# Batch 0 turned to kappa rows by DMA transposes in place of identity products, in a Fourier mixing layer followed by an expert layer on one core

## The chip, the cores and the metric

The kernel runs on 1 core of one Trainium2 chip. The metric is the device time of one execution in microseconds, as the median of several runs. Before the change it is 860.0 us.

## The reference

Input `x` has 8 batches of 3008 positions with 256 channels. Each batch goes through a Fourier transform along the positions, a complex product with two 256x256 matrices, a soft threshold and the inverse transform. The 24064 rows that come out go through a dense layer of 2048 hidden units with a squared ReLU. Cut to what matters:

```python
X = np.fft.rfft(x, axis=1)                 # x: 8 x 3008 x 256
Yr = Xr @ w_r - Xi @ w_i + b_r
Yi = Xr @ w_i + Xi @ w_r + b_i
Yr = np.sign(Yr) * np.maximum(np.abs(Yr) - 0.01, 0.0)   # Yi likewise
y = np.fft.irfft(Yr + 1j * Yi, n=3008, axis=1)
h = y.reshape(24064, 256) @ w_in           # 256 x 2048
g = s * np.maximum(h, 0.0) ** 2 + b
out = g @ w_out                            # 2048 x 256
```

## The kernel before

**The transform as products.** 3008 is split as 94 x 32 (`N1`, `N2`). A first small product over the 94 (matrix `A_t`) gives 96 "kappa" rows for each of the 32 positions n2. Then comes a product over the 32 n2 for each of 24 pairs of frequencies (`F_t`), the mixing with the weights (`W_t`, `W_g`), the threshold, the product back (`T_t`), and a last product over the 96 kappa rows (`C_t`), which gives the 94 again. Between these products the data must be turned, so that the index to be summed lies on the partitions. TensorE (PE) does the products into PSUM, ScalarE (ACT) and VectorE (DVE) copy them out ("evictions"), GpSimd (POOL) issues the loads of `x` and of the expert weights, and SyncE (SP) issues all other transfers.

**Batch 0, the prologue** (`first_batch`, line 351). Nothing else can fill the engines yet, so batch 0 has a path of its own. Its first step (line 362) leaves `ut` in SBUF, with channels on the partitions. Then it goes in 12 steps (ec, u): two halves of the channels (ec, 128 each) by `U` = 6 groups of four pairs. Step i emits, in this order: `mix` of step i (line 411, eviction to g at 418 or 421), `fwd_dft` of step i-1 (line 442, threshold at 447 on ACT and 449 on DVE, giving z), `inv_dft` of step i-2 (line 460, eviction into `vt`). `vt` holds, for a half, channels on the partitions and 96 kappa values for each of 32 n2. When the six steps of a half are through, `turn(ec, k)` turns eight n2 at a time to kappa rows: eight products of a 128x96 block of `vt` with an identity (line 474), and one eviction of 96x1024 elements into `vs[0]`. `last_dft(ec, n2)` (line 489) then does the last product for eight n2 and evicts it to `yt`, which the expert layer reads. The four turns of the first half lie among the steps of the second; the four of the second half stand behind them:

```python
            k = i - U - 2
            if 0 <= k < 4:
                turn(0, k)
            if 0 <= k - 1 < 4:
                last_dft(0, 8 * (k - 1))
            if i >= 2 * U:
                some(3)
...
        for k in range(4):
            turn(1, k)
            some(1)
            if k:
                last_dft(1, 8 * (k - 1))
        last_dft(1, 24)
        return more
```

`some(n)` emits n of the 16 units of batch 1's first step (`s1_units`, line 550; products at 564), each four products and one eviction of 128x384 elements into `u`. Ten of the 16 are emitted here, and the other six among tile 0 of the expert layer (`schedule(0, 10, more)`, line 865).

**Batches 1 to 7.** Here the result `u` of the first step is turned by DMA transposes, one for each half of the channels, as soon as eight units are through (line 574, issued by SP): `us` <- `u`, 24 blocks of 128x128. `s23_units` (line 582) goes on from there with `fwd_unit` (products at 597), mixing (612, 626), threshold (631 to 638), small copies through `ring`, `inv_unit` (656), and a way through memory (`vd`, line 665, read back as `vs`, line 672). `s4_units` (line 693) is the last product.

**The expert layer.** 48 tiles of at most 512 rows are worked through in order. Each has 16 slots; a slot emits `first_mm` (line 758, ReLU on ACT at 765 and the square on DVE at 772 or ACT at 769) and its share of `second_mms` of the tile before (line 829, scaled and stored at 839 and 784). The work of the later batches is laid into these slots by hand in `plan`: `s23_units(1)` starts at slot 24, that is in the middle of tile 1; slot 17 loads `x` of batch 2, gated by a one-element copy that waits for the first transposed half of batch 1 (line 185).

**What sets the order.** Each engine works through its own instructions in the order of the program, and waits for semaphores. PSUM has three pools of two buffers: `psh` (two banks each, `two_banks`), `psf` (`one_bank`) and `psa` (`other_bank`). `evac` (line 155) gives each eviction to ACT or DVE, whichever has the smaller sum of estimated work so far; the sums are set to zero after `first_batch`. The loads of the prologue run in this order on POOL: `x` of batch 0; then, gated by the arrival of the table `T_c`, `x` of batch 1, `w_in` (line 266) and `w_out` (line 267).

Of the kernel before, what the change touches and what calls it, by code (L numbers as in the profile page):

```python
# [9 lines left out]
F16 = mybir.dt.float16  # L10
F32 = mybir.dt.float32
# [3 lines left out]
P = 128  # L15
N1 = 94
N2 = 32
# [79 lines left out]
def kernel(  # L97
# [13 lines left out]
    nc = tc.nc  # L111
    B, S, D = x.shape
    N = S
    assert N == N1 * N2 and D == 2 * P and B % 2 == 0
    DC = D // P
# [3 lines left out]
    HW = N2 // 2  # L119
# [7 lines left out]
    sel = np.zeros((P, P))  # L127
    sel[0, :64] = 1.0
    sel[64, 64:] = 1.0
    E_d = nc.inline_tensor(np.eye(P).astype(np.float16), name="identity").ap()  # L130
    S_d = nc.inline_tensor(sel.astype(np.float16), name="bias_sel").ap()

    cpool = ctx.enter_context(tc.tile_pool(name="consts", bufs=1))
    bigpool = ctx.enter_context(tc.tile_pool(name="big", bufs=1))
# [12 lines left out]
    tpool = ctx.enter_context(tc.tile_pool(name="tp", bufs=2))  # L147
# [7 lines left out]
    def evac(dst, src, cols, scale=None):  # L155
        ta, td = 0.17 + cols / 1200.0, 0.15 + cols / 960.0
        if load["act"] + ta <= load["dve"] + td:
            load["act"] += ta
            if scale is None:
                return None, nc.scalar.copy(out=dst, in_=src)  # L160
            return None, nc.scalar.mul(out=dst, in_=src, mul=scale)
        load["dve"] += td
        if scale is None:
            return nc.vector.tensor_copy(out=dst, in_=src), None
        return nc.vector.tensor_scalar_mul(out=dst, in0=src, scalar1=scale), None

    def two_banks():
        return hpool.tile([P, 2, 512], F32, name="psh", tag="psh")

    def one_bank():  # L170
        return fpool.tile([P, 512], F32, name="psf", tag="psf")

    def other_bank():
        return apool.tile([P, 512], F32, name="psa", tag="psa")
# [38 lines left out]
        nc.sync.dma_start(out=st, in_=w.rearrange("(c p) e -> p c e", p=P))  # L213
        w_st.append(st)

    b_g = cpool.tile([P, 2, D], F32, name="b_g")
    nc.vector.memset(b_g, 0.0)
    for r in (0, 64):
        for i, bv in enumerate((b_r, b_i)):
# [2 lines left out]
    F_c = first_c[:, 0].rearrange("p (q r k) -> p q r k", q=NPAIR, r=2)  # L222
    T_c = first_c[:, 1].rearrange("p (q k) -> p q k", q=NPAIR)
    F_2 = [first_c[:, 2 + i].rearrange("p (q k) -> p q k", q=H) for i in range(2)]
    b_h = cpool.tile([P, D], F16, name="b_h")
    nc.vector.memset(b_h, 0.0)

    for i, bv in enumerate((b_r, b_i)):
        nc.gpsimd.dma_start(out=b_h[64 * i : 64 * i + 1], in_=bv.unsqueeze(0))
    sel_t = cpool.tile([P, P], F16, name="sel_t")  # L230
    eye_t = cpool.tile([P, P], F16, name="eye_t")
    C_t = cpool.tile([96, 96], F16, name="C_t")

    b_st = rpool.tile([P, 2, D], F32, name="b_st", tag="rt")
# [12 lines left out]
    def emit_load_inverse():  # L247
        nc.sync.dma_start(
            out=F_c[:, H:].rearrange("p q r k -> p q (r k)"), in_=F_d[:, H:]
        )  # L250
        t_load = nc.sync.dma_start(out=T_c, in_=T_d)
        with tc.issue_after(t_load.ins):
            nc.sync.dma_start(out=eye_t, in_=E_d)
            nc.sync.dma_start(out=C_t, in_=C_d)
            for i, bv in enumerate((b_r, b_i)):
                nc.sync.dma_start(out=b_st[:, i], in_=bv.unsqueeze(0).to_broadcast([P, D]))
            nc.sync.dma_start(out=s_bc, in_=moe_s.unsqueeze(0).to_broadcast([P, 1]))
            nc.sync.dma_start(out=bb_bc, in_=moe_b.unsqueeze(0).to_broadcast([P, 1]))
# [67 lines left out]
    def sum_w_out():  # L326
        acc = opool.tile([P, 2, D], F32, name="acc", tag="ost")
        nc.gpsimd.tensor_tensor(
            out=acc, in0=w_out_t[:, 0:2], in1=w_out_t[:, 2:4], op=ALU.add
        )  # L330
        for q in range(4, MC, 2):
            nc.gpsimd.tensor_tensor(out=acc, in0=acc, in1=w_out_t[:, q : q + 2], op=ALU.add)
        nc.gpsimd.tensor_tensor(out=w_sum, in0=acc[:, 0], in1=acc[:, 1], op=ALU.add)

    def make_bias():
        ps = other_bank()
        nc.tensor.matmul(ps[:, 0:D], ones, w_sum, start=True, stop=True)
        for j in range(2):
            nc.scalar.activation(
                out=bias_bc[:, j], in_=ps[:, 0:D], func=AF.Copy, scale=bb_bc  # L340
            )

    us = {}
    vs = {}
    ring = []
# [5 lines left out]
    def first_batch():  # L351
# [3 lines left out]
        for g in range(N2 // 4):  # L355
            c, h = divmod(g, 2)
            for dc in range(DC):
                ps = one_bank() if dc else two_banks()[:, 0]
                with tc.issue_after(last_pe.ins):
                    for j in range(4):  # L360
# [4 lines left out]
                            start=True, stop=True,  # L365
# [32 lines left out]


        U = NPAIR // 4  # L400
        vt = bigpool.tile([P, DC, N2, 96], F16, name="vt", tag="corr")
        gs = {}
        zt = {}
        g_last = [None]
# [1 line left out]
        def mix(ec, u):  # L406
            ps = two_banks().rearrange("p h (j r e) -> p (h j) r e", j=2, r=2)
            for j in range(4):
                q = 4 * u + j
                for dc in range(DC):  # L410
                    nc.tensor.matmul(  # L411
                        ps[:, j], ut[:, dc, 4 * q : 4 * q + 4, :],
                        W_t[:, dc, :, ec * P : (ec + 1) * P],
                        start=(dc == 0), stop=(dc == DC - 1),
                    )
            g = vpool.tile([P, 4, 2, P], F16, name="g0", tag="v")
            if u % 3 == 1:
                g_last[0] = nc.scalar.copy(out=g, in_=ps)
                load["act"] += 1.02
            else:  # L420
                g_last[0] = nc.vector.tensor_tensor(
                    out=g, in0=ps,
                    in1=b_g[:, :, ec * P : (ec + 1) * P].unsqueeze(1).to_broadcast([P, 4, 2, P]),
                    op=ALU.add,
                )
                load["dve"] += 1.2
            gs[(ec, u)] = g
# [40 lines left out]

        vs[0] = vspool.tile([P, N2, D], F16, name="vs", tag="vs")

        def turn(ec, k):
            ps = two_banks()
            for j in range(8):
                nc.tensor.matmul(
                    ps[0:96, j // 4, (j % 4) * P : (j % 4) * P + P],
                    vt[:, ec, 8 * k + j, :], eye_t, start=True, stop=True,
                )
            evac(
                vs[0][0:96, 8 * k : 8 * k + 8, ec * P : (ec + 1) * P],
                ps[0:96].rearrange("p h (j e) -> p (h j) e", e=P), 1024,  # L480
            )

        yt = yts[0] = ypool.tile([P, DC, N2, 96], F16, name="yt", tag="yt")

        def last_dft(ec, n2):

            ps = [one_bank(), other_bank()]
            for j in range(8):
                nc.tensor.matmul(
                    ps[j // 4][:, (j % 4) * 96 : (j % 4) * 96 + 96],  # L490
                    vs[0][0:96, n2 + j, ec * P : (ec + 1) * P], C_t,
                    start=True, stop=True,
                )
            for i in range(2):
                evac(
                    yt[:, ec, n2 + 4 * i : n2 + 4 * i + 4, :],
                    ps[i][:, 0:384].rearrange("p (j n) -> p j n", n=96), 384,
                )

        more = s1_units(1, True)  # L500

        def some(n):
            for _ in range(n):
                if more:
                    more.pop(0)()

        steps = [(ec, u) for ec in range(DC) for u in range(U)]
        for i in range(2 * U + 2):
            if i < 2 * U:
                mix(*steps[i])  # L510
            if 0 <= i - 1 < 2 * U:
                fwd_dft(*steps[i - 1])
            if 0 <= i - 2 < 2 * U:
                inv_dft(*steps[i - 2])
            k = i - U - 2
            if 0 <= k < 4:
                turn(0, k)
            if 0 <= k - 1 < 4:
                last_dft(0, 8 * (k - 1))
            if i >= 2 * U:  # L520
                some(3)
            if i == 0:
                with tc.issue_after(g_last[0].ins):
                    place_t(0)
            if i == 1:
                with tc.issue_after(g_last[0].ins):
                    place_f(1)
            if i == 2:
                with tc.issue_after(g_last[0].ins):
                    place_f_2(1)  # L530
            if i == 3:
                with tc.issue_after(g_last[0].ins):
                    place_t(1)
            if i == 9:

                gate = nc.gpsimd.tensor_copy(out=low[0:1, 0, 0:1], in_=vt[0:1, 1, 0, 0:1])
                with tc.issue_after(gate.ins):
                    make_w_g()
                    make_bounds()
                    sum_w_out()  # L540
        for k in range(4):
            turn(1, k)
            some(1)
            if k:
                last_dft(1, 8 * (k - 1))
        last_dft(1, 24)
        return more


# [302 lines left out]
    def schedule(start, span, units):  # L852
        for i, u in enumerate(units):
            plan.setdefault(start + (i * span) // len(units), []).append(u)

    more = first_batch()
    load.update(act=0.0, dve=0.0)
    def load_x_2():
# [3 lines left out]
    for i, tl in enumerate(tiles):  # L862
        if tl[0] == "main" and tl[2] == 0 or tl[0] == "wide" and tl[2] == (0, 0):
            mark[tl[1]] = i * MC
    schedule(0, 10, more)
    plan.setdefault(15, []).append(make_bias)
    plan.setdefault(17, []).append(load_x_2)
    schedule(24, 42, s23_units(1))
# [1 line left out]
    for b in range(2, B):  # L870
        s0, s1, s2 = mark[b - 2], mark[b - 1], mark[b]
        p = s1 - s0
        schedule(s0 + 40, p - 48, s1_units(b))
        p = s2 - s1
# [47 lines left out]
```

## Time and profile before

| what | value |
|---|---|
| runs | 859.21, 860.0, 860.82 us; median 860.0 |
| the profiled execution | 860.82 us, of which its span is 859.0 us |
| granted TensorE clock | 0.994 of full speed on average |
| busy share of the span | PE 97%, PE weight loads 71%, DVE 81%, ACT 74%, POOL 5% |
| chain that ended last | PE 86%, DMA 7%, ACT 3%, DVE 2% |
| identity products (line 474) | 64, of 219 ns each, overlapping; 8 in 0.61 us |
| evictions of the turns | 6 on ACT of 1013 ns, 2 on DVE of 1214 ns |
| transposes of line 574 | 14; SP held for 3.6 to 15.8 us each, median 4.8 |
| first expert product | at 49.1 us |

"Span" is the time from the first to the last instruction of the core; the profiled execution takes 1.8 us beyond it. A busy PE is not a PE at its peak, since products are pipelined and their ends modelled. The shares are means over stages with different limits. "Wait" is idle time of an engine with what released it. SP's own time is not in the busy table; how long one instruction holds SP's queue is read in the timeline.

### The profile page before, as it was taken

How to read it: one execution, taken by the hardware profiler on the slowest of the kernel's cores; microseconds unless marked ns; L12 is line 12 of the kernel's file. 1: busy time of each engine (PE TensorE's matmuls, PEld its weight loads, DVE VectorE, ACT ScalarE, POOL GpSimd, SP SyncE). 2: the span in 40 equal slices, each digit the busy share in tenths (PEclk: the TensorE clock that was granted, in tenths of full speed). 3: DMA queues.
4: the chain of work that ended last, by engine and by line, in shares of the span. 5: the costliest groups of instructions: out<-in, count | busy, mean ns of one | idle time of the engine just before them, and what ended most of it. 6: DMA issues, size and time to landing. Idle time of an engine off the chain costs nothing.

```text
span 859.0 us, 17659 instructions
## 1 busy us (share of the span) xinstructions
PE 833.9 (97%) x6981; PEld 608.6 (71%) x6981; DVE 694.0 (81%) x1025; ACT 638.9 (74%) x858; POOL 46.5 (5%) x72
## 2 busy tenths in 40 slices
PE   8899999999999999799989999999999999999997
PEld 6766777777777766477767777777767777766765
DVE  6888987888878987588968888788887888776674
ACT  5887877788778877478767777687877878766673
POOL 5440000000000001000000000000000000000000
PEclk9999999999999999899999999999999999999999
DMA  7862368122851359422682226813262132411111
GB/s 171 151 117 73 86 157 179 41 77 72 198 128 46 101 148 121 78 73 81 120 168 69 71 82 140 181 38 89 79 171 63 50 87 81 128 33 38 38 44 50
DMA packets 123829, 84.11 MB, mean 98 GB/s; under 512 B 52070, under 2 KB 118634, under 8 KB 122402
## 3 DMA queue, kind: packets, MB, share of 16 engines
q1 hardware_dynamic: 117298, 68.56, 32.4%
q0 software_dynamic: 6448, 14.42, 10.4%
q8 instruction: 55, 0.90, 0.4%
q14 instruction: 28, 0.23, 0.1%
HBM read 41.53 MB, written 35.65 MB: 90 GB/s over the span
## 4 chain that ended last, share of the span: by engine, by line
PE 86%; DMA 7%; ACT 3%; DVE 2%; issue 1%; POOL 0%; SPq 0%; DVEq 0%; ACTq 0%; POOLq 0%
PE psa L829 36%; PE psh L758 35%; PE psf L626 4%; DMA us<-u 3%; PE psf L597 2%; PE psf L612 2%; PE psf L656 2%; PE psf L564 2%; PE psf L707 2%; DMA vs<-vd 1%; DMA x<-in_x_dram 1%; ACT rt L765 1%; DMA ring<-ring 1%; DMA vd<-v 1%; PE psh L411 1%
## 5 line engine op out<-in xcount | busy, mean ns | idle before, releaser
L765 ACT ACTIVATE rt<-psh 128x1024 f32<-128x1024 f32 (+2 forms) x384 | 387.3, 1010 | 117.9 <-PE psh L758 115.6
L772 DVE TENSOR_TENSOR gt<-rt 128x1024 f16<-128x1024 f32 (+2 forms) x320 | 383.8, 1204 | 98.0 <-ACT rt L765 97.0
L829 PE MATMUL psa<-w_out_t,gt 128*128 128x256 f16 (+1 forms) x3024 | 455.8, 273 | 0.0
L829 PEld LDWEIGHTS <-gt 128*128 128x128 f16 (+1 forms) x3024 | 301.3, 101 | 185.3 <-issue 1.4
L758 PE MATMUL psh<-yt,w_in 128*128 128x512 f16 (+1 forms) x1344 | 398.2, 378 | 0.2 <-ACT rt L765 0.2
L758 PEld LDWEIGHTS <-w_in 128*128 128x128 f16 x1536 | 138.0, 98 | 14.3 <-issue 0.5
L839 DVE SCALAR_TENSOR_TENSOR ost<-psa,s_bc,bias_bc 128x512 f32<-128x512 f32 (+2 forms) x97 | 71.1, 733 | 14.3 <-PE psa L829 10.5
L769 ACT ACTIVATE gt<-rt 128x1024 f16<-128x1024 f32 (+2 forms) x64 | 67.4, 1054 | 1.0
L160 ACT CAST v<-psf 128x512 f16<-128x512 f32 x80 | 46.6, 583 | 22.5 <-PE psf L656 22.4
L160 ACT CAST xf<-psf 128x512 f16<-128x512 f32 x77 | 45.0, 586 | 19.7 <-PE psf L597 19.7
L631 DVE TENSOR_TENSOR ring<-psf,s 128x512 f16<-128x512 f32 x84 | 57.5, 685 | 2.6 <-PE psf L626 2.4
L758 PE MATMUL psh<-tail,w_in 128*128 128x512 f16 (+1 forms) x192 | 52.6, 355 | 0.0
L160 ACT CAST u<-psf 128x384 f16<-128x384 f32 x85 | 40.8, 481 | 13.6 <-PE psf L564 12.8
L626 PE MATMUL psf<-W_g,xf 128*128 128x256 f16 x336 | 50.4, 272 | 0.1
L160 ACT CAST yt<-psf 128x480 f16<-128x480 f32 (+2 forms) x68 | 34.9, 532 | 13.7 <-PE psf L707 13.5
L189 POOL DMA_DIRECT2D x<-in_x_dram x36 | 18.8, 527 | 454.2 <-PE psf L564 452.7
L597 PE MATMUL psf<-F_t,us 128*128 128x128 f16 x336 | 33.3, 221 | 8.4 <-DMA us<-u 8.4
L637 DVE TENSOR_TENSOR ring<-ring,high 128x512 f16<-128x512 f16 x84 | 35.5, 423 | 2.3
L638 DVE TENSOR_TENSOR ring<-ring 128x512 f16<-128x512 f16 x84 | 35.6, 423 | 2.2
L636 DVE TENSOR_TENSOR ring<-ring,low 128x512 f16<-128x512 f16 x84 | 35.4, 422 | 1.7
L707 PE MATMUL psf<-C_t,vs 96*128 96x96 f16 x448 | 33.9, 208 | 2.5 <-DMA vs<-vd 2.4
L564 PEld LDWEIGHTS <-x 94*128 94x128 f16 x448 | 30.8, 98 | 7.2 <-issue 3.4
(89 smaller groups left out, 518.2 us busy)
## 6 DMA issues: line engine op xcount, KB each, us to landing
out_dram<-ost SPq DMA_DIRECT2D x152, 128.0 KB
vd<-v SPq DMA_DIRECT2D x42, 256.0 KB
vs<-vd SPq DMA_DIRECT2D x14, 768.0 KB
x<-in_x_dram POOLq DMA_DIRECT2D x28, 376.0 KB, 6.8
ring<-ring SPq DMA_DIRECT2D x280, 32.0 KB
out_dram<-ost SPq DMA_DIRECT2D x16, 120.0 KB
x<-in_x_dram POOLq DMA_DIRECT2D x8, 188.0 KB, 6.4
out_dram<-ost SPq DMA_DIRECT2D x12, 112.0 KB
```

Source lines behind the costliest of these rows:

```text
L160: return None, nc.scalar.copy(out=dst, in_=src)
L564: nc.tensor.matmul(ps[:, j * 96 : j * 96 + 96], x16[(b, c)][0:N1, lo : lo + P], A_t[0:N1, :], start=True, stop=True,)
L597: nc.tensor.matmul(ps[:, :, dc, j, :], us[b][:, 2 * i + j, dc * P : (dc + 1) * P], F_t[:, 2 * i + j, :], start=True, stop=True,)
L626: nc.tensor.matmul(ps[:, r, :], xt[:, 2 - r, dc], W_g[:, dc, r], start=(dc == 0), stop=(dc == DC - 1),)
L631: nc.vector.tensor_tensor(out=t, in0=ps, in1=hold[i // 2][:, i % 2].unsqueeze(1).to_broadcast([P, 2, D]), op=ALU.add,)
L707: nc.tensor.matmul(ps[:, j * 96 : (j + 1) * 96], vs[b][0:96, n2 + j, ec * P : (ec + 1) * P], C_t, start=True, stop=True,)
L758: nc.tensor.matmul(o, w_in_t[dc][:, mc * P : (mc + 1) * P], r, start=(dc == 0), stop=(dc == DC - 1),)
L765: nc.scalar.activation(out=rt[:, :, 0:w], in_=ps[:, :, 0:w], func=AF.Relu)
L769: nc.scalar.activation(out=gt[:, :, 0:w], in_=rt[:, :, 0:w], func=AF.Square)
L772: nc.vector.tensor_tensor(out=gt[:, :, 0:w], in0=rt[:, :, 0:w], in1=rt[:, :, 0:w], op=ALU.mult)
L829: nc.tensor.matmul(ps[0:size, h, :], gts[(ti, mc // 2)][:, mc % 2, sub * size : (sub + 1) * size], w_out_t[:, mc, :], start=(mc == 0), sto ...
L839: nc.vector.scalar_tensor_tensor(out=ost[0:size, 0:k], in0=ps[0:size, 0:k], scalar=s_bc[0:size], in1=bias_bc[0:size, 0:k], op0=ALU.mult, o ...
```

## The change

`turn` no longer uses TensorE. It issues two DMA transposes on SP for each half of the channels, 16 n2 each, from `vt` straight into `vs[0]`. The source block must be 128 wide for this, so `vt` gets 128 instead of 96 columns for each n2, and the padding is set to zero by a memset on POOL at the start. To make room, the identity is no longer loaded, and three small constants (`b_g`, `b_h`, `sel_t`) move to a pool that is used only later. The transposes of the first half are emitted once its six steps are through, and those of the second likewise. The calls of `last_dft(0, ...)` stand one step later than before, at i = 10 to 13. All 16 units of batch 1's first step are now emitted in the prologue: twelve behind the last step, and four among the calls of `last_dft(1, ...)`. The diff, without the lines that only move constants:

```diff
+    vt = bigpool.tile([P, DC, N2, P], F16, name="vt", tag="corr")
+    nc.gpsimd.memset(vt[:, :, :, 96:P], 0.0)
...
-        vt = bigpool.tile([P, DC, N2, 96], F16, name="vt", tag="corr")
...
-        def turn(ec, k):
-            ps = two_banks()
-            for j in range(8):
-                nc.tensor.matmul(
-                    ps[0:96, j // 4, (j % 4) * P : (j % 4) * P + P],
-                    vt[:, ec, 8 * k + j, :], eye_t, start=True, stop=True,
-                )
-            evac(
-                vs[0][0:96, 8 * k : 8 * k + 8, ec * P : (ec + 1) * P],
-                ps[0:96].rearrange("p h (j e) -> p (h j) e", e=P), 1024,
-            )
+        def turn(ec):
+
+            for k in range(2):
+                nc.sync.dma_start(
+                    out=vs[0][:, HW * k : HW * k + HW, ec * P : (ec + 1) * P],
+                    in_=vt[:, ec, HW * k : HW * k + HW].rearrange("p n k -> p (n k)"),
+                    transpose=True,
+                )
...
-            k = i - U - 2
-            if 0 <= k < 4:
-                turn(0, k)
-            if 0 <= k - 1 < 4:
-                last_dft(0, 8 * (k - 1))
-            if i >= 2 * U:
-                some(3)
+            if i - 1 in (U, 2 * U):
+                turn((i - 1) // U - 1)
+            if 0 <= i - U - 4 < 4:
+                last_dft(0, 8 * (i - U - 4))
...
+        some(12)
         for k in range(4):
-            turn(1, k)
+            last_dft(1, 8 * k)
             some(1)
-            if k:
-                last_dft(1, 8 * (k - 1))
-        last_dft(1, 24)
         return more
...
-    schedule(0, 10, more)
+    assert not more
```

More of the change, by code (lines that the diff above doesn't have):

```diff
@@ L129 @@
     sel[64, 64:] = 1.0
-    E_d = nc.inline_tensor(np.eye(P).astype(np.float16), name="identity").ap()
     S_d = nc.inline_tensor(sel.astype(np.float16), name="bias_sel").ap()
@@ L214 @@
         w_st.append(st)
-    b_g = cpool.tile([P, 2, D], F32, name="b_g")
+    b_g = tpool.tile([P, 2, D], F32, name="b_g", tag="tail")
     nc.vector.memset(b_g, 0.0)
@@ L224 @@
     F_2 = [first_c[:, 2 + i].rearrange("p (q k) -> p q k", q=H) for i in range(2)]
-    b_h = cpool.tile([P, D], F16, name="b_h")
+    sb_t = tpool.tile([P, P + D], F16, name="sb_t", tag="tail")
+    sel_t, b_h = sb_t[:, 0:P], sb_t[:, P:]
     nc.vector.memset(b_h, 0.0)
@@ L229 @@
         nc.gpsimd.dma_start(out=b_h[64 * i : 64 * i + 1], in_=bv.unsqueeze(0))
-    sel_t = cpool.tile([P, P], F16, name="sel_t")
-    eye_t = cpool.tile([P, P], F16, name="eye_t")
     C_t = cpool.tile([96, 96], F16, name="C_t")
@@ L252, in emit_load_inverse @@
         with tc.issue_after(t_load.ins):
-            nc.sync.dma_start(out=eye_t, in_=E_d)
             nc.sync.dma_start(out=C_t, in_=C_d)
```

## The prediction

> **What bounds the kernel now.** I read the page first: span, busy shares, chain of waits.
>
> ```profile
> span 859.0 us, 17659 instructions
> PE 833.9 (97%) x6981; PEld 608.6 (71%) x6981; DVE 694.0 (81%) x1025; ACT 638.9 (74%) x858; POOL 46.5 (5%) x72
> ...
> PE 86%; DMA 7%; ACT 3%; DVE 2%; issue 1%; POOL 0%; SPq 0%; DVEq 0%; ACTq 0%; POOLq 0%
> ```
>
> TensorE sets the time over the whole span. But the change touches only batch 0's prologue, so I read that stretch by itself (columns: stretch, length, busy PE, PEld, DVE, ACT, POOL, clock, DMA share, GB/s).
>
> ```profile
> 30.00:35.00 5.00, 4.58 (x64) 4.01 (x63) 3.90 (x5) 4.12 (x7) 2.49 (x3) 1.00 1.28 197
> 35.00:40.00 5.00, 4.93 (x73) 4.47 (x72) 4.77 (x7) 4.41 (x9) 3.63 (x5) 1.00 0.65 90
> 40.00:45.00 5.00, 3.54 (x59) 2.94 (x56) 4.47 (x10) 3.92 (x9) 4.69 (x5) 1.00 0.02 5
> 45.00:50.00 5.00, 4.49 (x75) 3.58 (x73) 4.12 (x7) 4.80 (x8) 3.33 (x4) 1.00 0.40 76
> ```
>
> From 30 to 50 us no engine is the bound alone: PE, DVE and ACT each work 70 to 99% and pass PSUM banks round. The DMA queues are full until 37 us and empty from 38 to 48. After 70 us PE is busy without a gap, so what counts is how much later or earlier PE enters that state. Next I read the transposes that the kernel already has (line 574, 24 blocks of 128x128 each), in the timeline:
>
> ```profile
> 46.88 3.78 SPq L574 DMA_TRANSPOSE us<-u  x1
> ...
> 52.60 1.00 POOL L185 COPY x<-us 1x1 f16<-1x1 f16 x2 [4.04 <-DMA us<-u]
> ...
> 56.10 9.38 SPq L574 DMA_TRANSPOSE us<-u  x1
> ...
> 67.55 0.51 PE L597 MATMUL psf<-F_t,us 128*128 128x128 f16 x6 [1.77 <-DMA us<-u]
> ```
>
> With empty queues one transpose holds SP 3.8 us and lands 5.7 us after its issue; beside the load of x it lands after 11.4 us, and PE idles 1.8 us for it.
>
> **What is removed.** The identity products and their evictions:
>
> ```profile
> L474 PE MATMUL psh<-eye_t,vt 128*96 128x128 f16 x64 | 4.9, 219 | 0.0
> ...
> L160 ACT CAST vs<-psh 96x1024 f16<-96x1024 f32 x6 | 6.1, 1013 | 0.1
> ...
> L164 DVE CAST vs<-psh 96x1024 f16<-96x1024 f32 x2 | 2.4, 1214 | 0.5 <-PE psh L474 0.5
> ```
>
> That is 4.9 us of PE and 8.5 us of ACT and DVE together, 4.3 us if it splits evenly. None of it comes out as such: what stands in its place are waits for transfers.
>
> **What is added.** Four transposes of 16 blocks on SP, two for each channel half (ec), with nothing but loads ahead of them there. By the free row the data starts 1.2 us after issue, 24 blocks take 3.7 us and the release 0.7 us. So 16 blocks take 2.4 us: one lands 4.4 us after issue (1.2+2.5+0.7), a second behind it 2.4 us later.
>
> *First pair.* Its input, `vt` of ec 0, is complete at 31.0 us (ACT's eviction of 30.43, which the change does not move), so it is issued at 31.1. The queues are then full with the load of w_out:
>
> ```profile
> q0 software_dynamic: 2069, 1.19, 131.2%
> ...
> q0 software_dynamic: 365, 1.21, 86.2%
> q1 hardware_dynamic: 721, 0.18, 19.3%
> ```
>
> The first line is 31 to 37.4 us, the others 57.3 to 64.7 us, where a transpose (q1) ran beside the load of x (q0): two transpose packets passed for each packet of the load. w_out's packets are small, 3.1 ns each (6.4 us / 2069); a transpose packet of 256 bytes alone takes 0.9 ns (287 GB/s from 64.8 to 66.8 us). Two for one gives 512 bytes in 4.9 ns, 105 GB/s, so 0.52 MB takes 5.0 us and lands at 38.0. One for one gives 64 GB/s, and landing at 39.9, after w_out is through. Scaling the contended 11.4 us by 16/24 gives 38.7. I take 39.0. The ends are 35.5 (free row) and 43.0 (the worst row: issued at 332.06, waited for until 350.01, 17.9 us x 16/24).
>
> PE is ready for it sooner. In the changed program `last_dft(0, 0)` stands right behind `inv_dft` of step 8. Without the turns, PE gets there at about 35.4: DVE's g of step 8 ends at 32.4 as before, then z 0.68, g 1.22, z 0.68 give 35.0, and `inv_dft` 0.4. So PE stands 3.6 us, and behind it stand the mixes of step 11, the products of steps 10 and 11, and on DVE, whose next instruction is the eviction of `last_dft(0, 0)`, z of step 9. This wait is new; the identity products had none like it.
>
> *Second pair.* From 39.0 the chain to the last `vt` is: product 0.4, on DVE eviction 0.55, z 0.68, g 1.22, z 0.68 (42.5), `fwd_dft` 0.5, relu on ACT 0.7, two evictions of `last_dft` on DVE until 44.4, z 0.68, `inv_dft` 0.4, eviction 0.7: 46.4 with small gaps, against 44.6 now. The pair is issued then, on empty queues, and lands at 50.7 and 53.1. The twelve units of batch 1's first step that now stand there (12 x 0.52 us of eviction on two engines, 3.1 us) cover it until about 50.0. Behind the second landing stand four groups of `last_dft` and two units, 2.1 us of PE, before the expert matmuls of tile 0 run on: 55.3; first ReLU out at 56.9, first square 57.0, third 59.4. Before, the third square started at 55.1. Tile 0 is paced by these squares (8 in 9.2 us from 55.13), so it runs 4.3 us late. This already counts the six units that move from tile 0's slots into the prologue.
>
> *What comes back.* SP frees from the pair at 51.3, transposes batch 1's halves at 51.3 and 56.1, and the second lands near 62; PE asks for it at 65.8 + 4.3 = 70.1. So the 1.8 us stall at 67.55 goes. What would be late next is x of batch 2, gated by the first half (57); needed only 16 slots after that point.
>
> **At nothing:** the identity's load (SP idle until 46.9), the moved constants, and the memset of `vt`'s padding: 2048 elements where 1536 took 1.35 us, so 1.8 us, on a POOL that waits 5.95 us there for the tables; without this cover 1.8 us would delay w_out. From 70 us on the program is the same but for which engine takes some evictions: 0, within plus or minus 1.
>
> **Sum:** +4.3 - 1.8 = +2.5. The profiled execution took 860.82 (span 859.0 and 1.8 around it), 0.82 over the median of 860.0: 863.3 on its own basis, 862.5 on the median's.
>
> **Rules weighed.** The Trainium skill, "VectorE: DVE Perf Modes", section The three transpose paths, gives the crossbar 1309 ns for a 128x128 block against 390 ns on TensorE and advises TensorE where PSUM will do; that speaks against the change. The trace has 24 blocks in 5.7 us, 0.24 us each; by the page's figure, if blocks ran one after another, the 64 blocks would take 84 us and the kernel some 60 us longer, an estimate I do not follow.
>
> PE's clock after a stall:
>
> ```profile
> 346.00:347.00 1.00, 0.00 (x0) 0.00 (x0) 1.00 (x2) 0.00 (x0) 0.00 (x0) 1.00 1.20 23
> 347.00:348.00 1.00, 0.29 (x1) 0.10 (x1) 0.46 (x1) 0.00 (x0) 0.00 (x0) 0.55 1.17 261
> ...
> 353.00:354.00 1.00, 1.00 (x6) 0.54 (x5) 0.29 (x1) 0.73 (x2) 0.00 (x0) 0.54 0.00 0
> ```
>
> Idle from 343.1, PE fell to half clock about 4 us later and stayed so through 3.9 us of work; the 1.8 us gap at 66 us cost no clock. My 3.6 us lies just short of 4: I take 0, and up to 2 in the range. The skill's "TensorE: Matmul & The Clock Gate", Part 1, sets the idle window at about 3.4 us, free-running; by that the gap could trip it, and the sum would be up to 2 us more.
>
> **Rivals.** (1) The first pair lands in time, before 35.4, and nothing stalls: `vt` is complete at 43.2, the last landing is 49.9, tile 0 runs 1.1 late, and with the stall gone the kernel is 0.7 us faster, 859.3. Each us of landing after 35.4 costs one; the turn from gain to loss is 36.5. For it: the free row. Against: 197 GB/s from 30 to 35 us. (2) Starved as at 332.06, where x and a transpose held each other up: landing at 43.0, +6.5, and the clock surely halved, +1 to 2: 868. Against: w_out's packets are small. (3) The hole of 343 to 350 us, 6.6 us of waiting for one transpose plus half clock, comes out otherwise because evictions change engine: plus or minus 4, 856 to 866. Its transfers stand in the same order in the changed program, which speaks against it.
>
> **Chances.** Forecast 0.52, its own range 860.5 to 865; rival 1 0.25, rival 2 0.11, rival 3 0.12. The range for 8 in 10 reaches from 858.0 to 867.0. About 0.2%, 1.7 us, is what a measurement of this kernel can tell from no change. Faster by more: 0.18, from a third of rival 1, half of rival 3 and a little of the rest. Slower by more: 0.56, from two thirds of the forecast's spread, rival 2 and half of rival 3, rounded up for waits not seen. Between: 0.26.
>
> **What would show it.** The first `last_dft` idles on the DMA of `vs<-vt` until about 39 us; the second pair is issued near 46.4; the first square of tile 0 starts near 57; no wait on us<-u near 67 to 70; equal stretches after 75 us, shifted by 2.5. It is wrong if the first pair lands by 36, if PE's clock column shows 0.5 around 40, or if the second half of batch 1 is waited for again.

## The result, and the profile after

The changed kernel takes 884.4 us (median of four runs, 882.2 to 890.6), the kernel before 859.6 in the same comparison: a ratio of 1.030, with a 95% interval of 1.024 to 1.036. It is slower by 24.8 us where 2.5 were forecast, and outside the range. The profiled execution took 886.1, of which its span is 884.3; it is 25.3 above the profiled execution before. The page of the changed kernel, in the lines that answer to those of before:

```profile
span 884.3 us, 17541 instructions
PE 838.5 (95%) x6917; PEld 609.7 (69%) x6917; DVE 691.5 (78%) x1019; ACT 635.3 (72%) x856; POOL 47.7 (5%) x73
...
PE 83%; DMA 10%; ACT 3%; issue 2%; DVE 1%; POOL 1%; SPq 0%; DVEq 0%; ACTq 0%; POOLq 0%
```

PE has 64 products less and is busy for 4.6 us longer, which already hints at a lower clock; the share of DMA on the chain rises from 7 to 10%. Next the prologue in stretches of five us (stretch, length, busy PE, PEld, DVE, ACT, POOL, clock, DMA share, GB/s):

```profile
35.00:40.00 5.00, 1.14 (x16) 0.81 (x13) 0.64 (x2) 2.24 (x4) 3.77 (x4) 0.81 1.39 165
40.00:45.00 5.00, 1.32 (x12) 1.13 (x13) 0.78 (x2) 0.46 (x1) 3.68 (x4) 0.50 1.25 155
...
55.00:60.00 5.00, 2.10 (x24) 1.89 (x24) 1.72 (x4) 1.61 (x4) 0.00 (x0) 0.52 1.33 163
```

Before, PE, DVE and ACT worked 4.4 to 4.9 of the 5 us from 35 to 40. Now PE and DVE stand, the clock falls to half, and the queues, empty from 38 us on before, are full until 44. What PE stands for is in the timeline of PE; the bracket at the end of a line is the idle time before the instruction and what ended it:

```profile
43.68 0.50 PE L486 MATMUL psf<-C_t,vs 96*128 96x96 f16 x4 [7.54 <-DMA vs<-vt]
...
56.46 0.50 PE L486 MATMUL psf<-C_t,vs 96*128 96x96 f16 x4 [1.70 <-DMA vs<-vt]
60.75 0.50 PE L486 MATMUL psf<-C_t,vs 96*128 96x96 f16 x4 [2.19 <-DMA vs<-vt]
...
88.97 0.82 PE L589 MATMUL psf<-F_t,us 128*128 128x128 f16 x6 [10.55 <-DMA us<-u]
```

Line 486 (before 489) is `last_dft`, line 589 (before 597) `fwd_unit` of batch 1. There are four waits for transposes, 22.0 us together, where the kernel before had one of 1.8 in this stretch. The largest is not for the transposes that were added, but for the second half of batch 1, which was transposed before as well. SP's queue and POOL's show what it ran beside:

```profile
52.01 4.40 SPq L474 DMA_TRANSPOSE vs<-vt  x2
56.59 4.79 SPq L566 DMA_TRANSPOSE us<-u  x1
```

```profile
63.94 3.61 SPq L566 DMA_TRANSPOSE us<-u  x1
```

```profile
64.24 2.18 POOL L188 DMA_DIRECT2D x<-in_x_dram  x4 [0.31 <-POOL x L184]
```

The second half (63.94) is issued 0.3 us before the four loads of x of batch 2 (64.24). It lands at 88.9, 25 us later; the median landing of those four loads is 23.8 us after issue. Both crawl.

**Where the 25 us come in.** I follow one instruction through all kernels, the ReLU of the expert layer on ACT: by how much is the first one late (tile 0), the 13th (tile 1, behind the place where batch 1 is first asked for), the 33rd (tile 4), and the last? All profiled executions are set against the one before (51.1, 69.4, 119.8 and 847.0 us).

| kernel | median us | ratio to before (95%) | first | 13th | 33rd | last |
|---|---|---|---|---|---|---|
| the change | 884.4 | 1.030 (1.024 to 1.036) | +13.1 | +23.0 | +22.8 | +25.3 |
| x2_gate_second | 873.2 | 1.017 (1.012 to 1.021) | +13.9 | +11.3 | +11.2 | +8.3 |
| half0_identity | 863.9 | 1.006 (1.003 to 1.009) | +4.9 | +2.9 | +3.0 | +1.6 |
| half1_identity | 874.1 | 1.016 (1.012 to 1.021) | +10.4 | +13.1 | +13.1 | +15.2 |
| w_out_after_pair | 869.7 | 1.013 (1.008 to 1.017) | +9.2 | +6.8 | +6.7 | +8.3 |
| copies_before | 851.5 | 0.992 (0.989 to 0.994) | +0.5 | +3.2 | +3.2 | -9.4 |
| copies_after | 859.9 | 1.002 (1.000 to 1.003) | +8.5 | +12.6 | +12.8 | +0.3 |
| held_38 | 859.6 | 1.001 (0.999 to 1.003) | +10.3 | +11.7 | +11.7 | -0.9 |
| held_38_awake | 859.5 | 1.000 (0.998 to 1.002) | +7.8 | +10.7 | +11.5 | -1.2 |
| copies_met | 860.7 | 1.003 (1.001 to 1.005) | +7.5 | +11.8 | +11.4 | +3.2 |

So the change loses 13.1 us before tile 0, 9.9 at the start of batch 1, and 2.3 behind that. The last column belongs to one execution and need not be the median's: x2_gate_second was 869.0 in its profiled run and 873.2 in the median.

### The profile page after: what moved, and what is told of

It is laid out like the page before. It is cut to its first block, busy times and chain, and to the rows that moved or that the text cites. A ratio compares the mean times of both kernels' runs of the same rounds, so it can differ in the third digit from the quotient of the medians.

```text
span 884.3 us, 17541 instructions
## 1 busy us (share of the span) xinstructions
PE 838.5 (95%) x6917; PEld 609.7 (69%) x6917; DVE 691.5 (78%) x1019; ACT 635.3 (72%) x856; POOL 47.7 (5%) x73
## 4 chain that ended last, share of the span: by engine, by line
PE 83%; DMA 10%; ACT 3%; issue 2%; DVE 1%; POOL 1%; SPq 0%; DVEq 0%; ACTq 0%; POOLq 0%
PE psa L821 34%; PE psh L750 34%; DMA us<-u 5%; PE psf L618 4%; PE psf L589 2%; DMA vs<-vt 2%; PE psf L604 2%; PE psf L648 2%; PE psf L699 2%; PE psf L556 2%; ACT rt L757 1%; DMA vs<-vd 1%; DMA vd<-v 1%; DMA x<-in_x_dram 1%; DMA first_c<-dft_inv 0%
## 5 line engine op out<-in xcount | busy, mean ns | idle before, releaser
L159 ACT CAST xf<-psf 128x512 f16<-128x512 f32 x81 | 47.3, 585 | 29.3 <-PE psf L589 29.2
L159 ACT CAST v<-psf 128x512 f16<-128x512 f32 x76 | 44.4, 584 | 23.3 <-PE psf L648 23.2
L589 PE MATMUL psf<-F_t,us 128*128 128x128 f16 x336 | 33.4, 223 | 17.9 <-DMA us<-u 17.9
L159 ACT CAST u<-psf 128x384 f16<-128x384 f32 x82 | 39.3, 481 | 12.9 <-PE psf L556 11.9
L159 ACT CAST yt<-psf 128x480 f16<-128x480 f32 (+2 forms) x73 | 37.1, 524 | 14.5 <-PE psf L699 13.7
L595 DVE TENSOR_TENSOR xf<-xf 128x256 f16<-128x256 f16 x84 | 23.7, 287 | 22.8 <-ACT xf L159 22.3
L589 PEld LDWEIGHTS <-us 128*128 128x128 f16 x336 | 26.2, 100 | 20.9 <-DMA us<-u 18.6
L629 DVE TENSOR_TENSOR ring<-ring,high 128x512 f16<-128x512 f16 x84 | 35.5, 423 | 2.3
L630 DVE TENSOR_TENSOR ring<-ring 128x512 f16<-128x512 f16 x84 | 35.5, 423 | 2.1
L628 DVE TENSOR_TENSOR ring<-ring,low 128x512 f16<-128x512 f16 x84 | 35.4, 422 | 1.7
```

The lines of the kernel that those rows point to most:

```text
L589: nc.tensor.matmul(ps[:, :, dc, j, :], us[b][:, 2 * i + j, dc * P : (dc + 1) * P], F_t[:, 2 * i + j, :], start=True, stop=True,)
L629: nc.vector.tensor_tensor(out=m, in0=m, in1=high, op=ALU.min)
L630: nc.vector.tensor_tensor(out=t, in0=t, in1=m, op=ALU.subtract)
```

## The experiments

**Is the wait of 10.6 us a collision with x of batch 2?** Theory: the prologue's delay pushes the second half of batch 1 to the moment at which x of batch 2 is loaded. That load is let go by the landing of the *first* half. (In the change its gate, a copy on POOL, starts at 63.40. The trace names the last unit of batch 1's first step as its last release, since that unit reads the buffers that x is loaded into; the first half had landed 0.1 us before.) Rival: the transpose is late in any case, because it stands behind four more transposes in SP's queue. In x2_gate_second the load is let go by the second half instead:

```diff
-        emit_load_x(2, us[1][0:1, 0, 0:1])
+        emit_load_x(2, us[1][0:1, 0, P : P + 1])
```

> The changed kernel, with the load of x of batch 2 gated by the second transposed half of batch 1 instead of the first, so that it can't run beside that transpose. Theory A (two collisions: the first pair of transposes meets the load of w_out, and the second half of batch 1 meets the load of x, 25 us from issue to landing where an empty queue takes 5.7): the 10.6 us wait of PE for us<-u near 80 us and the half clock after it go, the first ReLU of tile 0 stays where it is (64.2 us), total 874 us (871 to 877). Theory B (transposes issued one behind another are slow by themselves, whatever else is on the queues): the second half still takes over 15 us, total 882 to 886.

Measured: 873.2 us, 11.3 less than the change. The waits of PE in the first 110 us (in all, times, longest), of the changed kernel:

```profile
PE psf L486 <- DMA vs<-vt: 11.4, 3, 7.5
PE psf L589 <- DMA us<-u: 10.6, 1, 10.6
```

and of x2_gate_second:

```profile
PE psf L486 <- DMA vs<-vt: 12.7, 3, 8.5
```

Nothing but the time of a load was moved; the wait on us<-u is gone, and the 13th ReLU is 11.7 us earlier. The collision is shown. The 13 us ahead of tile 0 are left as they were.

**Which pair costs what?** half0_identity turns the first channel half with the identity as before and only the second with transposes; half1_identity does it the other way round and lays six units of batch 1 among tile 0 again. Lines that load the identity or place those units are left out here:

```diff
 # half0_identity
-            if i - 1 in (U, 2 * U):
-                turn((i - 1) // U - 1)
-            if 0 <= i - U - 4 < 4:
-                last_dft(0, 8 * (i - U - 4))
+            if i - 1 == 2 * U:
+                turn(1)
+            k = i - U - 2
+            if 0 <= k < 4:
+                turn_pe(0, k)
+            if 0 <= k - 1 < 4:
+                last_dft(0, 8 * (k - 1))
 # half1_identity: instead
+            if i - 1 == U:
+                turn(0)
...
+            turn_pe(1, k)
```

> The changed kernel with the first half of batch 0 (ec 0) turned by identity products as before, the second half by transposes. Theory A: the 7.5 us wait before the first last_dft and the half clock of 38 to 48 us go, so tile 0 starts some 8 us earlier than in the changed kernel (first ReLU near 56); the second pair lands 4.1 and 6.7 to 8.5 us after issue, as there; the collision of the second half of batch 1 with x stays, because it is issued right beside that load; total 872 us (867 to 878). Theory B: each pair costs about half of the loss, total 872 too, but the pair of ec 1 then lands as late after its issue as the first pair did, 11 us.

Measured: 863.9 us. One wait for vs<-vt is left, ahead of the second pair:

```profile
50.18 0.50 PE L500 MATMUL psf<-C_t,vs 96*128 96x96 f16 x4 [3.02 <-DMA vs<-vt]
```

With the first pair gone, the second half of batch 1 is issued at 56.09, in front of x, and no wait on us<-u comes in the prologue. A collision that I had counted on here did not happen. The second pair alone, on queues that are nearly empty, makes the 13th ReLU 2.9 us late and costs 0.6% in all (0.3 to 0.9%): at its lower end what I had given to the whole change.

> The changed kernel with the second half of batch 0 (ec 1) turned by identity products, with the units of batch 1 spread as before (six of them among tile 0); the first half by transposes. Theory A: the first pair waits behind w_out as in the changed kernel (lands 11 to 12 us after issue, PE idle 7 us, half clock), tile 0 starts 7 to 9 us later than before (first ReLU 58 to 60); the second half of batch 1 is issued some 9 us after the first, when x is already on its way, and costs 1 to 3 us as before; total 868 us (865 to 872). Theory B: two transposes in a row instead of four, so half of the loss, 872.

Measured: 874.1 us, so the first pair is the dear one. Its wait, 10.4 us at 46.18, is even longer than in the change, and the delay then brings a meeting with x along:

```profile
79.35 0.82 PE L607 MATMUL psf<-F_t,us 128*128 128x128 f16 x6 [3.19 <-DMA us<-u]
```

Here the transpose of the second half is issued at 66.48, behind all four loads of x (64.16 to 66.27), and PE gets it 12.9 us later, in place of the 25 of the change.

**Does the first pair wait behind w_out?** In w_out_after_pair the load of w_out is not issued at 20 us; a one-element copy on POOL holds it back until the first pair has landed.

```diff
+    def emit_load_w_out(first):
+        gate = nc.gpsimd.tensor_copy(out=w_out_t[0:1, 0, 0:1], in_=first)
...
+                    emit_load_w_out(vs[0][0:1, HW, 0:1])
```

> The changed kernel with the load of w_out held back until the second transpose of the first pair has landed. Theory A: the pair is issued near 32 us when x of batch 1 and w_in are just through, lands 4.5 to 6 us after issue, PE waits under 1.5 us for it and keeps its full clock; first ReLU of tile 0 at 55 to 58 us instead of 64.2; the collision of the second half of batch 1 with x stays in some form; total 874 us (868 to 879). Theory B: the first transpose still lands over 9 us after its issue, total 882 to 886.

Measured: 869.7 us. Its timeline of PE:

```profile
37.36 0.34 PE L490 MATMUL psf<-C_t,vs 96*128 96x96 f16 x4 [1.74 <-DMA vs<-vt]
53.25 0.50 PE L490 MATMUL psf<-C_t,vs 96*128 96x96 f16 x4 [6.36 <-DMA vs<-vt]
```

Without w_out ahead of it the first pair, issued at 31.47, is there at 37.4, and 7.5 us of waiting become 1.7. But w_out, issued at 41.0 and landed at 51.7, now meets the second pair (6.4 us), and the wait for us<-u near 350 us, 4.1 before, is 8.3. The load starves whichever pair it stands beside; moving it moves the wait. The collision with x, which I had expected to stay, does not come: the second half is issued at 60.04, 1.3 us ahead of x, and PE does not wait for it.

**Is it the crossbar or the queue?** "Crossbar" stands here for the way that a transposing transfer takes. Two kernels put plain copies of the same bytes, from SBUF to SBUF in 256-byte packets on the same queue, in the place of *all* DMA transposes: copies_before in the kernel before (14 of them), copies_after in the changed one (18). The blocks are not transposed there.

```diff
-                    in_=u[:, dc].rearrange("p k n -> p (k n)"),
-                    transpose=True,
+                    in_=u[:, dc].rearrange("p (q a) n -> p q (a n)", a=4),
 # copies_after as well
-                    in_=vt[:, ec, HW * k : HW * k + HW].rearrange("p n k -> p (n k)"),
-                    transpose=True,
+                    in_=vt[:, ec, HW * k : HW * k + HW],
```

> The kernel before with each of its 14 DMA transposes replaced by a plain copy from SBUF to SBUF on the same queue at the same place: as many packets of 256 bytes, nothing is turned, so from batch 1 on it computes something else. It is the base for copies_after. Theory X (a transpose through the crossbar is held up by every other packet on any of the 16 engines; a plain copy is not): PE's waits for us<-u (8.4 us) fall under 3, total 849 to 856. Theory Q (small packets queue behind the loads, turned or not): waits and time as before, 857 to 861.

> The changed kernel with all 18 transposes replaced by plain copies of the same packets on the same queue (nothing is turned, so the result is another). Theory X: the first pair, beside the load of w_out, lands 5 to 7 us after its issue instead of 11.7, no holes of 1.4 us, PE waits for it 1 to 3 us instead of 7.5; the second half of batch 1 beside the load of x lands in under 14 us instead of 25; first ReLU of tile 0 at 55 to 58 (changed kernel 64.2); total 855 to 863. Theory Q: first pair 11 to 12 us, second half of batch 1 over 20 us, total 880 to 888.

Measured: 851.5 and 859.9 us. With copies the change costs 8.3 us, with transposes 24.8. The first pair is late with copies too (copies_after, timeline of PE):

```profile
43.09 0.50 PE L485 MATMUL psf<-C_t,vs 96*128 96x96 f16 x4 [6.13 <-DMA vs<-vt]
```

It is issued at 32.26, and its first packet is served at about 36.4, as with the transposes (31.99, about 36.0). So the start of the first pair is held up by what stands in the queues, not by transposing. Two things come with the transposes alone. First, a hole. In the changed kernel, from 59.0 to 60.4 us, transposes filled the queues and almost nothing moved (the same columns as in the stretches above):

```profile
59.00:60.00 1.00, 0.00 (x0) 0.00 (x0) 0.00 (x0) 0.14 (x1) 0.00 (x0) 0.50 1.92 10
```

The queues count as busy (1.92), and 10 GB/s pass. The hole begins beside a 16 KB packet of instruction fetch at 58.75; from 41.4 to 42.8 there is another, beside a fetch at 40.9. copies_after has a 16 KB fetch in the middle of its copies at 58 us as well and moves 219 GB/s through it. Other kernels with transposes have such holes as well: x2_gate_second at 59.9 and half1_identity at 75.4 us, each 0.2 to 0.3 us after such a fetch begins, but w_out_after_pair also one at 33.3, with no such fetch near. That the fetch is the cause is only argued. Second, copies_before, which is 0.8% faster than the kernel before: the waits on us<-u of 343 to 350 us and the hole at 440 are gone there, and 3.1 us of waiting on us<-u in the prologue are all that is left.

copies_after has the collision too: its second half is issued at 64.08, beside the first load of x at 64.00, and PE gets it 15.0 us later:

```profile
64.08 0.59 SPq L565 DMA_DIRECT2D us<-u  x1
...
79.06 0.56 PE L587 MATMUL psf<-F_t,us 128*128 128x128 f16 x7 [3.58 <-DMA us<-u]
```

copies_met makes sure of the meeting, and so repeats it: it holds that copy back until x is let go.

```diff
+            if g == N2 // 4 - 1 and (b, dc) != (1, 1):
...
     def load_x_2():
+        u = hold_u[(1, 1)]
+        nc.gpsimd.tensor_copy(out=u[0:1, 1, 0, 0:1], in_=us[1][0:1, 0, 0:1])
+        nc.sync.dma_start(
+            out=us[1][:, :, P : 2 * P],
+            in_=u[:, 1].rearrange("p (q a) n -> p q (a n)", a=4),
+        )
         emit_load_x(2, us[1][0:1, 0, 0:1])
```

> copies_after with one thing moved: the plain copy of the second half of batch 1 (768 KB, 256-byte packets) is held back by a one-element copy on GpSimd until the first half has landed, so that it is issued at the same time (about 64 us) as the four loads of x of batch 2, as in the changed kernel, where the DMA transpose of that half took 25 us beside them (issued 63.94, landed 88.9, wait of 10.6 us). Queue theory (small packets share the queues with the large packets of the load, whatever they do): the plain copy crawls too, lands 18 to 27 us after its issue, at 82 to 91 us, the matmuls on us<-u wait 4 to 11 us in the prologue (3.6 us in copies_after), and the kernel takes 860 to 867 us against 859.9. Crossbar theory (only transposes are held up, packet by packet, by the load): the plain copy lands 7 to 14 us after its issue, before it is asked for at about 79 us, the wait is at most 3.6 us and the kernel takes 856 to 861 us.

Measured: 860.7 us. The copy is issued at 63.03, x at 62.88, and PE gets it at 77.8 after a wait of 3.8 us. These 14.8 us lie between the two forecasts; they and the wait are nearly those of copies_after (15.0 and 3.6). The plainest sign is the traffic. First copies_met, then the changed kernel, each with x and the second half under way:

```profile
68.00:72.00 4.00, 4.00 (x29) 2.41 (x27) 4.00 (x5) 3.53 (x4) 0.00 (x0) 1.00 1.07 212
72.00:76.00 4.00, 1.95 (x15) 1.17 (x12) 4.00 (x4) 1.12 (x2) 0.00 (x0) 1.00 1.01 213
```

```profile
68.00:72.00 4.00, 4.00 (x22) 2.04 (x21) 4.00 (x4) 3.81 (x6) 0.00 (x0) 1.00 1.40 78
72.00:76.00 4.00, 4.00 (x26) 2.28 (x24) 4.00 (x5) 3.05 (x4) 0.00 (x0) 1.00 1.11 76
```

The same bytes, the same load and the same packet size of 256 bytes give 212 GB/s as copies and 77 as transposes. But a transpose beside x does not always crawl. In half1_identity, where it stands behind the loads of x, the queues carry as much as with copies:

```profile
68.00:72.00 4.00, 4.00 (x24) 2.13 (x22) 4.00 (x4) 3.76 (x6) 0.00 (x0) 1.00 1.05 204
```

And in half0_identity and w_out_after_pair, where it is issued 1.2 and 1.3 us ahead of x, PE does not wait for it at all. The crawl is seen once, in the change, where the transpose is issued 0.3 us ahead of x; the copies are issued 0.1 to 0.2 us behind the first load of x. So queueing makes the half late by some 9 us (14.8 against the 5.7 of a transpose on empty queues), and 10 more come in this one meeting. Whether they are due to the transposing or to the order and the 0.3 us between the two issues was not separated, and why the load slows down as well stays open. Splitting x into smaller packets beside a transpose was not measured, nor was the gate of x2_gate_second in the kernel before.

**What do the idle time and the half clock cost by themselves?** held_38 is copies_before with nothing changed but that the first `last_dft` waits for w_out (its other lines only keep the next step queued behind it); held_38_awake has 85 products without a use in the gap as well, which keep the clock up there.

```diff
+                if k == 1:
+                    nc.gpsimd.tensor_copy(out=vs[0][0:1, 0:8, 0:1], in_=w_out_t[0:1, 0:8, 0:1])
 # held_38_awake as well
+                    keep_awake(85)
```

> copies_before, in which the first last_dft of batch 0 must wait for w_out (one-element copies from w_out into vs[0]; the result is another), so that PE idles some 5 us from 34 us on, with nothing added to the DMA queues. The pair with held_38_awake prices the half clock. If it costs time by itself: clock 0.5 from about 38 to 48 us, first ReLU of tile 0 at 57 to 60. If only the wait counts: first ReLU at 55 to 56.5 (51.1 and 5 us).

> held_38 with 85 dummy products of ones (4.8 us) in the wait. If the half clock costs time: full clock throughout, first ReLU 2 to 4 us earlier than in held_38, total 1.5 to 4 us less. If not: within 0.5 us of held_38.

Measured: 859.6 and 859.5 us. PE stands for 5.8 us until 41.2 in held_38, and the kernel loses 8.1 us against copies_before, more than the wait itself: as much as the change costs with copies (8.3). The clock is at half for 6.8 us from 40.3 and for 3.4 more from 53.9; in held_38_awake it does not fall there. That is worth 2.6 us at the first ReLU, 1.0 at the 13th, 0.2 at the 33rd, and nothing in the total. But the gain does not vanish by itself. held_38_awake gets the second half of batch 1 at 77.34 us, 1.9 us before held_38 (79.22). Then its own clock falls, at 78.1 for 3.4 us, while PE has work, and held_38 keeps its clock there. The same group of four products, first in held_38_awake, then in held_38:

```profile
78.15 1.06 PE L834 MATMUL psa<-w_out_t,gt 128*128 128x256 f16 x4
```

```profile
80.00 0.60 PE L833 MATMUL psa<-w_out_t,gt 128*128 128x256 f16 x4
```

So the equal totals do not show that half clock costs nothing: one stretch of it was exchanged for another. What lies behind the difference of 2.3 us between the wait and the loss was not taken apart, and the change itself was not measured with its clock kept up.

None of the runs that compute the reference is faster than the kernel before, so there is no better version to show.

## Why the prediction was wrong

The sign was right and the mechanism of the first step too: a new wait of PE for a transfer that stands behind the load of w_out. The sum was short by 22.8 us on its own basis (25.3 against 2.5).

| step | predicted, us | measured, us |
|---|---|---|
| first pair issued | 31.1 | 31.99 |
| PE ready for it | 35.4 | 36.1 |
| first pair landed | 39.0 (35.5 to 43.0) | 43.7 |
| second pair issued | 46.4 | 52.0 |
| second pair landed | 50.7, 53.1 | 56.5, 60.8 |
| first ReLU out | 56.9 | 65.3 |
| batch 1's second half issued, landed | 56.1, 62 | 63.9, 89.0 |
| PE asks for it | 70.1 | 78.4 |
| half clock | none | from 38.1, 55.2 and 82.5, for 10.2 us each |

**Tile 0: +4.3 forecast, +13.1 measured.** The 56.9 of the forecast is the end of the first ReLU, which was 52.2 before: 4.7 us late, and 4.3 by the third square. Measured were 13.1 at the first ReLU and 12.7 at the third square (67.78 for 55.13). The 8.4 that are missing at the ReLU are 4.7 at the first landing, 1.0 from there to the issue of the second pair (8.4 for 7.4), 2.0 from its issue to its last landing (8.7 for 6.7, the hole among them), and 0.7 from there to the end of the ReLU (4.5 for 3.8).

The term that failed in the first landing is "the data starts 1.2 us after issue". That is the free row, put at the head of a transfer whose rate alone was then worked out for full queues. Beside w_out the first packet came 4.1 us after the issue. The hole at 41.4 and an issue 0.9 late make up most of the rest. Rival 2, landing at 43.0 with the clock halved, described the place rightly; its argument against itself, that w_out's packets are small, did not count, since small packets too stood in front.

**The stall of 1.8 us: "goes" forecast, +9.9 measured.** This is the largest error; 8.8 of it are the wait itself, 10.6 in place of 1.8. The half's last units stand among the calls of `last_dft(1, ...)`, behind the second pair, so a landing that is 7.7 us late (60.8 for 53.1) became an issue that is 7.8 late (63.9 for 56.1). The fault of the step is that x of batch 2 was looked at only as something that might itself be late ("what would be late next"), not as traffic. Its gate opens when the first half lands, at 57 by the forecast, 0.9 us after the issue of the second half: the two met by the forecast's own times, and the landing near 62 was that of free queues; it took 25 us, not 6. The prediction held both rows that price such a meeting, the 11.4 us of line 574 beside x and the 17.9 us from 332.06, and used them for the first pair alone. From 56.1 the second of them reaches to 74.0, past the 70.1 at which PE was to ask. x2_gate_second shows that 11 us hang on this one meeting.

**The clock: 0 forecast.** The clock fell, and earlier than the row of 343 us suggests: PE stood from 36.1, and half clock began at 38.1. The price of 0 is not borne out: held_38 against held_38_awake gives 2.6 us at the first ReLU, and their totals are equal only by the second fall described there. In the change, half clock (38.1 to 48.4, 55.2 to 65.4) lies in the stretches of the 1.0 and the 0.7 us of tile 0 above, which were not taken apart. Behind the wait for us<-u it lasts through 3.8 us of work on PE (88.97 to 92.73); half of that, 1.9 us, is an estimate of what it cost there, from the 1.06 and 0.60 us of the same group above. The Trainium skill's "TensorE: Matmul & The Clock Gate", Part 1, has the gate watch a free-running window of about 3.4 us; here half clock lasted 10.2 us three times, three such windows, and 6.8 and 3.4 in held_38. That section's table has half clock come after at least one idle window. The onsets here do not fit that: the fall at 38.1 came 2.0 us after PE's last product, and the one at 55.2 came 0.4 us after, with PE busy for 2.5 of the 3.4 us before it.

**From tile 1 on: 0 forecast, +2.3 measured.** Rival 3, the hole of 343 to 350 us: the waits there were 6.6 us in all and are 7.3, with half clock for longer, and the delay of 22.6 us before it stands at 28.2 behind it; the kernel before loses 3.8 of that at 440 us, where it has a hole of its own. At the hole alone the 5.6 us are more than the 4 of that rival; the 2.3 that remain in the end lie within it.

**The page that spoke against the change**, "VectorE: DVE Perf Modes" of the Trainium skill, was right in the verdict and not in the size: the 64 blocks did not take 84 us (in half0_identity 16 blocks were there 5.2 us after issue). What makes the transposes dear here is what they meet.

## What to carry to other kernels

Before a transfer is put on a queue, list every load that is under way from its issue to its landing, and price start and rate by a row that ran beside such a load; the price of a free queue is only the lower end, and the upper one can be far off: 24 blocks took 5.7 us alone and 11.4, 12.9 and 25 beside the same load of x. When a change delays a stretch, look at every load that is let go by an event inside it: the delay moves that load as well, and two transfers that used to follow each other may meet. A gate on the last transfer that must be through, rather than on the first, keeps them apart; here that was worth 11 us.

## What was not expected of the hardware

- A DMA transpose and a load of x, issued 0.3 us apart, slowed each other down far below what the queues can carry: 77 GB/s together, against 212 for the same bytes as plain copies beside the same load, and 204 for a transpose issued behind it (half1_identity).
- The transposes stood still for 1.4 to 1.5 us at a time, twice in this prologue, with some 10 GB/s moved while the queues counted as busy. In the traces with plain copies in their place no such hole was found.
- The fourteen transposes of the kernel before cost it 0.8% (0.6 to 1.1%) against plain copies of the same bytes; of the 7 us, 5.3 are waits of PE for us<-u (8.4 against 3.1).
- Half clock for 10.2 us of a prologue that mostly waits (held_38) cost 2.6 us at the first ReLU. It came back without a long gap: at 53.9 us there, with PE busy for 2.5 of the 3.4 us before.
